# Where the conversion of the weights runs: 24 steps in row 0 instead of 36, the rest over all of row 1, and one token group of channel work moved to row 2

## The chip, the cores and the metric

The kernel runs on one core of one Trainium2 chip. The metric is the device time of one execution in microseconds (us). Three runs of the kernel before took 1360.92, 1362.69 and 1366.38 us; the median, 1362.69 us, is what a change is compared with. One more execution was profiled: the program ran 1362.23 us and the profile spans 1360.1 us of it.

The core has five engines with an instruction queue each. PE is the matrix engine, DVE the vector engine, ACT the scalar engine with activation functions, POOL the general engine (GpSimd) and SP the engine that here only issues transfers (DMA). Each works through its queue in the order of the program. An instruction waits until the data and the buffers that it needs are free, and all that stands behind it on its engine waits too.

## The reference

The input is an attention block with 8 batch elements, 8 heads, 576 tokens and 64 numbers per head, followed by an MLP mixer:

```python
scores = scale * (q @ k.T)                          # per batch element and head, 576 x 576
scores = where(scores >= max(scores) - tau, scores, -1e9)
attn = softmax(scores)
x = heads side by side of (attn @ v)                # 8 x 576 x 512
u = x + (relu(x.T @ w_tok1) @ w_tok2).T             # mixing over the 576 tokens, width 256
out = u + relu(u @ w_ch1) @ w_ch2                   # mixing over the 512 channels, width 1536
```

q, k and v are float32. The four weight matrices are float64, and the kernel computes in float32, so it has to convert them on the chip. That conversion is what the change moves.

## The kernel before

**Rows and units.** A "row" is one batch element, `b` from 0 to 7. A row is cut into 18 "units", so that there are 144, and the main loop (from L572) takes one unit per turn; `u` is its number, so units 18 to 35 are row 1. A unit is 128 query rows of one pair of heads. For unit u the loop emits, spread over engines:

- `scores(u)` (L289): 8 matmuls into PSUM on PE (line L303), two maxima on DVE (L308), two small instructions on POOL that make the threshold (L309);
- `weigh(u)` (L312): threshold and exponential on ACT (L318, L325);
- `norm(u - 1)` (L329): two tiny DVE instructions (L332, L333) and two scalings on POOL (L336);
- for unit w = u - 2 the transposition of the attention weights. In row 0 that is `turn` on PE with copies on DVE and ACT (L354, L356). From row 1 on it is `turn_blocks` (L358): one DVE transpose in blocks of 32 x 32 (L366, tile T), and after every third unit 16 transfers that move the blocks to their places (L375, tile eT), all issued by SP;
- `values` (L392): attention times v (L410, L415, tile pv), once for every three units. From row 1 on it is emitted at the end of the unit two after the one in which the 16 transfers were issued, and so directly ahead of the next unit's scores on PE.

**The mixer as filling.** When a row's attention is complete, `push` (L537) appends its mixer work to a list `todo`: `token_mlp` (L427), then `channel_mlp` (L476) for groups of 256 tokens. A group has 12 steps `ch1` of the first layer (8 matmuls each in the records, L487) and, for each of its two blocks of 128 tokens, 4 steps `ch2` of the second layer (L499, L503, with a copy on DVE, L508, at the end). `fill(share)` (L524) takes steps from the list at fixed places in the next row's units, by their estimated costs: a unit may take `quota`. `push` sets the quota so that `KEEP` of the list's cost is left after a row: 45 after rows 1 to 7, `KEEP_FIRST` = 20 after row 0. Row 0's list has two groups. `push(0)` runs in unit 20, `push(1)` in unit 39.

**The conversion.** The weights are cut into 31 pieces of up to 128 x 512 numbers: 3 of w_tok1, 4 of w_tok2, 12 of w_ch1, 12 of w_ch2. Each piece is loaded as 64-bit words by SP (`load_piece`, L177) into one of 4 raw buffers, and converted by two ACT instructions (L192, L194), three DVE instructions (L202, L204, L208) and one POOL addition (L216), which also frees the raw buffer. The sequence is cut into 94 steps, `weight(n)` (L224): step 3i is the first DVE instruction of piece i with the POOL addition of piece i - 1 and the load of piece i + 3; steps 3i + 1 and 3i + 2 are the other two DVE instructions with the ACT instructions of piece i + 1. `weight_to(x)` makes steps until x are done. `need(i)` (L242) makes as many as a piece requires before a step of the mixer uses it.

**What sets the order.** The order on each engine is the order in which the loop emits instructions; nothing reorders them later. In a unit of row 0 weight steps come in two places, and the target grows by 2.25 steps a unit (L599, L634). From unit 18 on `weight(2)` stands in three places of a unit (L595, L623, L629): after `norm`, after `turn_blocks`, and after `weigh`:

```python
if b_now:
    weight(2)
else:
    weight_to(2.25 * (u - (1 if visit else 1.5)))
```

On SP the loads of weights, the loads of v and, in row 0, the loads of q and k (L105) stand in one queue with the 16 transfers of each group of three units. From row 1 on q and k are loaded from ACT's queue.

Of the kernel before, what the change touches and what calls it, by code (L numbers as in the profile page):

```python
# [9 lines left out]
F32 = mybir.dt.float32  # L10
# [7 lines left out]
P = 128  # L18
# [3 lines left out]
def kernel(  # L22
# [38 lines left out]
    NCC = DM // P  # L61
# [16 lines left out]
    ps_mm = None  # L78
# [7 lines left out]
    UB = 9 * NP // 2  # L86
# [81 lines left out]
    def load_piece(i):  # L168
        if i >= len(pieces):
            return  # L170
        dst, src = pieces[i]
        rows = dst.shape[0]
        n = 1
        for d in dst.shape[1:]:
            n *= d
        raw = raw_at[i % NRAW][0:rows, 0 : n * (2 if wide(i) else 1)].bitcast(src.dtype)
        nc.sync.dma_start(out=like(raw, dst), in_=src)  # L177
        if wide(i):
            words = raw.bitcast(U32).rearrange("p (n w) -> p n w", w=2)
            h2 = work.tile([P, WMAX], F32, tag="o", name=f"h2_{i}")[0:rows, 0:n]  # L180
            raws[i] = like(words[:, :, 0], dst), like(words[:, :, 1], dst), like(h2, dst)
        else:
            raws[i] = like(raw, dst)
# [4 lines left out]
    def on_scalar(i, part):  # L188
        if wide(i):
            lo, hi, h2 = raws[i]  # L190
            if part == 0:
                nc.scalar.activation(out=lo.bitcast(I32), in_=lo, func=AF.Copy, scale=2.0**-29)  # L192
            else:
                nc.scalar.activation(out=h2, in_=hi.bitcast(F32), func=AF.Abs)  # L194
# [17 lines left out]
    def on_gpsimd(i):  # L212
        if i >= 0:
            dst = pieces[i][0]
            if wide(i):
                nc.gpsimd.tensor_tensor(out=dst.bitcast(I32), in0=dst.bitcast(I32), in1=raws.pop(i)[0].bitcast(I32), op=ALU.add)  # L216
            else:
                nc.gpsimd.tensor_copy(out=dst, in_=raws.pop(i))
# [5 lines left out]
    def weight(n):  # L224

        nonlocal steps_done
        for k in range(steps_done, min(steps_done + n, 3 * len(pieces) + 1)):
            i, part = divmod(k, 3)
            if part == 0:
                on_gpsimd(i - 1)  # L230
                if i:
                    load_piece(i - 1 + NRAW)
            else:
                on_scalar(i + 1, part - 1)
            on_vector(i, part)
            steps_done = k + 1

    def weight_to(x):

        weight(max(int(x) - steps_done, 0))  # L240

    def need(i):  # L242

        weight(3 * i + 4 - steps_done)
# [32 lines left out]
    def in_blocks(b):  # L277
        return b > 0
# [197 lines left out]
    def channel_mlp(b, uT, i):  # L476

        s = {}
        n = min(GR, 2 * S - GR * i)

        def ch1(j):
            need(7 + j)
            if j == 0:
                s["g"] = work.tile([P, NJ, GR], F32, tag="g", bufs=1, name=f"g_{b}_{i}")
            ps = ps_mm.tile([P, GR], F32, tag="mm", name=f"c1_{b}_{i}_{j}")[:, 0:n]
            for c in range(NCC):
                nc.tensor.matmul(ps, lhsT=wc1[:, j, c, :], rhs=uT[:, c, GR * i : GR * i + n], start=(c == 0), stop=(c == NCC - 1))  # L487
            nc.scalar.activation(out=s["g"][:, j, 0:n], in_=ps, func=AF.Relu)  # L488

        def ch2(t, part):  # L490
            need(7 + NJ + 3 * part + 2)
            t0 = GR * i + P * t
            if part == 0:
                s["ps"] = ps_mm.tile([P, NCC, P], F32, tag="mm", name=f"c2_{b}_{i}_{t}")
            ps = s["ps"]
            flat = ps.rearrange("q c d -> q (c d)")
            if part == 0:
                for c in range(NCC):
                    nc.tensor.matmul(  # L499
                        ps[:, c, :], lhsT=uT[:, c, t0 : t0 + P], rhs=ident, is_transpose=True, start=(c == 0), stop=False, skip_group_check=True  # L500
                    )
            for j in range(3 * part, 3 * part + 3):
                nc.tensor.matmul(  # L503
                    flat, lhsT=s["g"][:, j, P * t : P * t + P], rhs=wc2[:, j, :], start=False, stop=(j == NJ - 1), skip_group_check=True
                )
            if part == 3:
                o = work.tile([P, DM], F32, tag="o", name=f"o_{b}_{i}_{t}")
                nc.vector.tensor_copy(out=o, in_=flat)  # L508
                nc.sync.dma_start(out=out[b : b + 2].rearrange("b s d -> (b s) d")[t0 : t0 + P, :], in_=o)

        return [(0.0067 * n, lambda j=j: ch1(j)) for j in range(NJ)] + [
            (2.6 if part else 3.0, lambda t=t, part=part: ch2(t, part)) for t in range(n // P) for part in range(4)
        ]

    KEEP = 45.0
    KEEP_FIRST = 20.0
    todo = deque()  # L520
    quota = 0.0
    credit = 0.0
# [14 lines left out]
    def push(b):  # L537
# [13 lines left out]
        for i in range(2) if b % 2 == 0 else range(2, (2 * S + GR - 1) // GR):  # L551
            todo.extend(channel_mlp(b - b % 2, uT, i))
        quota = (sum(c for c, _ in todo) - (KEEP if b else KEEP_FIRST)) / (UB - 1)

    prep(0)
    due = deque()
    b_now = 0
    LAG = 2

    def values_due(u):  # L560
        while due and due[0][0] <= u:
            _, b, p0, g = due.popleft()
            values(b, p0, g)
            if b == 0 and p0 == 0 and g == 2:
                return True
            if p0 == NP - 2 and g == 2:
                if not in_blocks(b):
                    return True
                push(b)
        return False  # L570

    for u in range(len(units) + LAG + 4):  # L572
        on = u < len(units)
        if u == UB:
            late.close()
            ps_mm = ctx.enter_context(tc.tile_pool(name="ps_mm", bufs=2, space=bass.MemoryType.PSUM))
        if on:
            b_now, p0, t = units[u]
            n = b_now * NP + p0
        w = u - LAG  # L580
        back = 0 <= w < len(units)
        if on:
            scores(u)

        last = False
        visit = False
        if due and not in_blocks(due[0][1]):
            visit = due[0][0] <= u
            last = values_due(u)
        elif early:  # L590
            early.popleft()[1]()
        if 0 < u <= len(units):
            norm(u - 1)
        if b_now:
            weight(2)  # L595
        else:


            weight_to(2.25 * (u - (1 if visit else 1.5)))  # L599
            if visit and on:  # L600
                weigh(u)
        while copies:
            copies.popleft()()
        if last and u < UB:
            early.extend(token_mlp(0, range(NP // 2))[0])
        elif last:
            push(0)
        if back:
            wb, wp, wt = units[w]
            if not in_blocks(wb):  # L610
                for i in range(3):
                    turn(w, i)
            if wt % GU == GU - 1:
                g = wt // GU
                if g < 2:
                    split_middle(wb * NP + wp + g)
                due.append((u + (2 if in_blocks(wb) else 1), wb, wp, g))
        if b_now:
            fill(0.4)
        if back and in_blocks(wb):  # L620
            turn_blocks(w)
        if b_now:
            weight(2)  # L623
        if on and (b_now or not visit):
            weigh(u)
        elif b_now:
            fill(0.6)
        if b_now:
            weight(2)  # L629
        elif u == 0:  # L630
            on_scalar(0, 0)
            on_scalar(0, 1)
        else:
            weight_to(2.25 * (u - 1))  # L634
        if on:


            when = {3: (2, 0, 2), 4: (2, 2, 4), 5: (2, 4, 6), 6: (2, 6, 8), 8: (3, 0, 3), 0: (1, 3, 6), 1: (1, 6, 8)}
            if u == 0:
                load_qk(1, (nc.sync, nc.sync), range(0, 3))  # L640
            if t in when:
                m, lo, hi = when[t]
                if n + m < len(pairs):
                    load_qk(n + m, (nc.scalar if b_now else nc.sync,) * 2, range(lo, hi))
            if t in (3, 7) and n + 2 + t // 4 < len(pairs):
                load_v(n + 2 + t // 4)
            if t == 2:
                prep(n + 1)
            if t == 7 and n + 2 < len(pairs):
                prep(n + 2)  # L650
        if due and in_blocks(due[0][1]):
            values_due(u)
# [31 lines left out]
```

## Time and profile before

| What | Value |
|---|---|
| median of 3 runs | 1362.69 us |
| span of the profiled execution | 1360.1 us |
| PE busy | 1315.2 us, 97% of the span |
| DVE, ACT, POOL busy | 575.3, 584.3, 353.6 us (42, 43, 26%) |
| row 0: start to the first scores of unit 18 | 0 to 99.76 us, PE busy 78.30 of the first 100 us |
| row 1: scores of unit 18 to scores of unit 36 | 99.76 to 240.55 us |
| conversion instructions on DVE (L202, L204, L208) | 31 each, the last begins at 187.2 us |
| channel layers, matmuls of L487 and L503 | 400.3 and 390.6 us busy |
| mean of one issue of a transfer of L375 (median) | 602 ns, 672 of them |
| such a transfer from its issue to landing (median) | 2.3 us |

The busy time of PE is modelled from the starts of pipelined matmuls, so that short waits inside a group of matmuls don't show as idle time; the length of a whole group (8 matmuls of scores take 1.24 us where nothing disturbs them) tells more. "Idle before" beside an instruction is the time that its engine sat before it, and the name behind the arrow is what came last by the profile, which need not be what was waited for.

### The profile page before, as it was taken

The numbers are of one execution on the slowest core, as the hardware profiler recorded it, in microseconds if no ns is written. First come the engines' busy times: TensorE is split into PE (matmuls) and PEld (weight loads), VectorE is DVE, ScalarE is ACT, GpSimd is POOL, SyncE is SP. The second block draws the span as 40 slices with busy tenths as digits, with TensorE's granted clock in tenths as the row PEclk, the third lists the DMA queues.
The fourth block names the chain that finished last, engine by engine and source line by source line (L and its number), as shares of the span: only waits on it lengthen the run. The fifth ranks groups of instructions, "written<-read, shape, count | busy, mean of one in ns | idle before, by whom it ended". The sixth has DMA issues, their size and how long they took to land.

```text
span 1360.1 us, 17717 instructions
## 1 busy us (share of the span) xinstructions
PE 1315.2 (97%) x6246; PEld 817.2 (60%) x6246; DVE 575.3 (42%) x1009; ACT 584.3 (43%) x1299; POOL 353.6 (26%) x683
## 2 busy tenths in 40 slices
PE   6888899999999999999999999999999999999998
PEld 4555556547474666655665566565756566576675
DVE  5878874445443434443333454434333443201000
ACT  6776664445454444543434445353434444120010
POOL 4666653222222222221212222222212222100000
PEclk9999999999999999999999999999999999999999
DMA  5434774545453533533244444435333442400000
GB/s 122 109 92 129 196 170 102 127 95 127 96 130 77 134 89 84 135 76 92 66 112 99 104 97 114 95 76 118 90 90 74 114 99 70 111 0 16 8 16 16
DMA packets 278871, 128.20 MB, mean 94 GB/s; under 512 B 200896, under 2 KB 271552, under 8 KB 278784
## 3 DMA queue, kind: packets, MB, share of 16 engines
q1 hardware_dynamic: 150176, 111.06, 32.0%
q10 hardware_dynamic: 128608, 16.01, 7.4%
q8 instruction: 50, 0.82, 0.3%
q14 instruction: 37, 0.30, 0.1%
HBM read 43.25 MB, written 9.44 MB: 39 GB/s over the span
## 4 chain that ended last, share of the span: by engine, by line
PE 89%; DVE 4%; DMA 2%; ACT 2%; issue 1%; SPq 1%; POOL 1%; ACTq 0%; DVEq 0%; POOLq 0%
PE c L503 28%; PE c L487 27%; PE sc L303 11%; PE pv L415 8%; PE t L453 5%; PE t L463 4%; PE pv L410 3%; DVE mx L308 2%; PE c L499 1%; PE tx L446 1%; PE tr L354 1%; ACT e L318 1%; SPq L375 1%; DMA eT<-T 1%; DMA lk<-in_k_dram 1%
## 5 line engine op out<-in xcount | busy, mean ns | idle before, releaser
L308 DVE TENSOR_REDUCE mx<-sc 128x1 f32<-128x576 f32 x288 | 204.5, 750 | 484.6 <-PE sc L303 484.6
L487 PE MATMUL c<-xT,wc 128*128 128x256 f32 (+1 forms) x1920 | 400.3, 362 | 0.1
L503 PE MATMUL c<-wc,g 128*128 128x512 f32 x864 | 390.6, 597 | 0.0
L487 PEld LDWEIGHTS c<-xT,wc 128*128 128x128 f32 x1920 | 334.4, 191 | 70.5 <-issue 31.5
L309 POOL TENSOR_SCALAR bias<-mx,toff 128x1 f32<-128x1 f32 x288 | 81.9, 284 | 781.2 <-DVE mx L308 724.3
L318 ACT ACTIVATE e<-sc,bias 128x576 f32<-128x576 f32 x288 | 199.4, 740 | 157.5 <-POOL bias L309 153.5
L503 PEld LDWEIGHTS c<-wc,g 128*128 128x128 f32 x864 | 157.4, 190 | 175.4 <-issue 173.7
L488 ACT ACTIVATE g<-c 128x256 f32<-128x256 f32 (+1 forms) x240 | 86.8, 362 | 321.4 <-PE c L487 308.6
L325 ACT ACTIVATE e<-e,ntau 128x576 f32<-128x576 f32 x288 | 221.1, 772 | 0.0
L336 POOL TENSOR_SCALAR e<-e,rr 128x576 f32<-128x576 f32 x288 | 214.6, 757 | 14.7 <-DVE rr L333 2.8
L303 PE MATMUL sc<-kT,qT 64*128 64x288 f32 (+1 forms) x1280 | 193.5, 441 | 11.9 <-DVE kT L285 7.2
L366 DVE STREAM_TRANSPOSE T<-e 128x1152 f32<-128x1152 f32 x126 | 172.1, 1366 | 5.8 <-DMA eT<-T 3.6
L303 PEld LDWEIGHTS sc<-kT,qT 64*128 64x128 f32 (+1 forms) x1280 | 106.2, 181 | 99.2 <-issue 61.8
L415 PE MATMUL pv<-eT,lv 128*64 128x384 f32 (+1 forms) x1024 | 136.2, 406 | 0.0
L415 PEld LDWEIGHTS pv<-eT,lv 128*64 128x64 f32 x1024 | 75.2, 137 | 49.3 <-issue 40.4
L508 DVE COPY o<-c 128x512 f32<-128x512 f32 x36 | 24.7, 687 | 169.7 <-PE c L503 169.7
L420 ACT COPY xT<-pv 128x384 f32<-128x384 f32 (+1 forms) x56 | 21.0, 400 | 166.2 <-PE pv L415 165.2
L463 PE MATMUL t<-w,a 128*128 128x288 f32 x256 | 73.6, 414 | 5.7 <-DVE xT L467 4.8
L453 PE MATMUL t<-x_sb,w 128*128 128x512 f32 (+1 forms) x180 | 73.4, 555 | 0.0
L467 DVE TENSOR_TENSOR xT<-xT,t 128x288 f32<-128x288 f32 x64 | 28.4, 448 | 86.6 <-PE t L463 86.0
L463 PEld LDWEIGHTS t<-w,a 128*128 128x128 f32 x256 | 45.5, 190 | 28.0 <-issue 11.7
L325 ACT ACTIVATION_READ_ACCUMULATOR e<-e,ntau 128x1 f32 x288 | 56.8, 197 | 0.0
(44 smaller groups left out, 547.2 us busy)
## 6 DMA issues: line engine op xcount, KB each, us to landing
eT<-T SPq DMA_DIRECT2D x672, 108.0 KB, 2.3
scratch<-in_moe_w_ch_dram SPq DMA_DIRECT2D x24, 512.0 KB, 3.8
lv<-in_v_dram SPq DMA_DIRECT2D x32, 288.0 KB, 3.5
out_dram<-o SPq DMA_DIRECT2D x36, 256.0 KB, 2.2
lk<-in_k_dram ACTq DMA_DIRECT2D x111, 72.0 KB, 2.7
lq<-in_q_dram ACTq DMA_DIRECT2D x106, 72.0 KB, 2.3
lq<-in_q_dram SPq DMA_DIRECT2D x22, 72.0 KB, 3.2
lk<-in_k_dram SPq DMA_DIRECT2D x17, 72.0 KB, 3.4
```

What stands on the lines that cost most here:

```text
L303: nc.tensor.matmul(sc[h][rows, f, 0:HS], lhsT=qT[r, cols], rhs=kT[r, HS * f : HS * f + HS], start=True, stop=True)
L308: nc.vector.tensor_reduce(out=mx[:, c], in_=sc[h][:, :, 0:HS], axis=AX.XY, op=ALU.max)
L318: nc.scalar.activation(out=eh, in_=sc[h][:, :, 0:HS], func=AF.Prelu, bias=bias[:, h : h + 1], scale=SCALE, alpha=STEEP)
L325: nc.scalar.activation(out=eh, in_=eh, func=AF.Exp, bias=ntau, accum_out=rs[:, h : h + 1])
L336: nc.gpsimd.tensor_scalar(out=eh, in0=eh, scalar1=rr[:, h : h + 1], scalar2=1.0, op0=ALU.mult, op1=ALU.mult)
L366: nc.vector.transpose(out=T[:, :, place, :].rearrange("p a (c x) -> p c a x", c=NK), in_=e.rearrange("p (c a x) -> p c a x", c=NK, a=4))
L415: nc.tensor.matmul(to[r], lhsT=lv[:, j, :], rhs=e[j], start=False, stop=(c == NI - 1), skip_group_check=True)
L453: nc.tensor.matmul(to, lhsT=w1[:, t, P * m : P * m + P], rhs=x_sb[:, t, cols], start=(t == 0), stop=(t == NT - 1))
L463: nc.tensor.matmul(to, lhsT=a[:, m, P * c : P * c + P], rhs=w2[:, m, HS * f : HS * f + HS], start=(m == 0), stop=(m == NTK - 1))
L487: nc.tensor.matmul(ps, lhsT=wc1[:, j, c, :], rhs=uT[:, c, GR * i : GR * i + n], start=(c == 0), stop=(c == NCC - 1))
L488: nc.scalar.activation(out=s["g"][:, j, 0:n], in_=ps, func=AF.Relu)
L503: nc.tensor.matmul(flat, lhsT=s["g"][:, j, P * t : P * t + P], rhs=wc2[:, j, :], start=False, stop=(j == NJ - 1), skip_group_check=True)
```

## The change

Four things are changed together.

1. Row 0 makes 1.75 steps a unit instead of 2.25, and stops at `WROW` = 24. The kernel before was at 36 when row 1 began.
2. In row 1 the three calls `weight(2)`, 6 steps a unit, become a target that grows by `WRATE` = 4 steps a unit, with its steps at the same three places: two steps after `norm`, one after `turn_blocks`, one after `weigh`. Step 94 is thus reached in unit 35 instead of unit 27.
3. `KEEP_FIRST` goes from 20 to 42, so that row 1 takes less of row 0's list: the first group of tokens is done in it, the second one later.
4. For group 0 of row 0 the second layer is sorted by weights: part 0 of both blocks of tokens, then part 1 of both, and so on, so that late pieces are needed late. For that both blocks hold a PSUM buffer at once, `s[t]` instead of `s["ps"]`.

```diff
-                s["ps"] = ps_mm.tile([P, NCC, P], F32, tag="mm", name=f"c2_{b}_{i}_{t}")
-            ps = s["ps"]
+                s[t] = ps_mm.tile([P, NCC, P], F32, tag="mm", name=f"c2_{b}_{i}_{t}")
+            ps = s[t]
...
+        last = [(t, part) for t in range(n // P) for part in range(4)]
+        if b == 0 and i == 0:
+            last.sort(key=lambda x: x[1])
         return [(0.0067 * n, lambda j=j: ch1(j)) for j in range(NJ)] + [
-            (2.6 if part else 3.0, lambda t=t, part=part: ch2(t, part)) for t in range(n // P) for part in range(4)
+            (2.6 if part else 3.0, lambda t=t, part=part: ch2(t, part)) for t, part in last
         ]
...
-    KEEP_FIRST = 20.0
+    KEEP_FIRST = 42.0
...
+    WROW = 24
+    WRATE = 4.0
...
         if b_now:
-            weight(2)
+            weight_to(WROW + WRATE * (u - UB))
         else:
-            weight_to(2.25 * (u - (1 if visit else 1.5)))
+            weight_to(min(1.75 * (u - (1 if visit else 1.5)), WROW))
...
         if b_now:
-            weight(2)
+            weight_to(WROW + WRATE * (u - UB + 0.4))
...
         if b_now:
-            weight(2)
+            weight_to(WROW + WRATE * (u - UB + 0.7))
...
         else:
-            weight_to(2.25 * (u - 1))
+            weight_to(min(1.75 * (u - 1), WROW))
```

## The prediction

> **What bounds the kernel now.** I read the page's slices first, then busy times by stretch, then the queues of SP, PE and DVE in order of time through row 1.
>
> ```profile
> PE   6888899999999999999999999999999999999998
> ...
> DVE  5878874445443434443333454434333443201000
> ...
> PEclk9999999999999999999999999999999999999999
> ```
>
> A slice is 34 us. PE is short of work only in the first five slices, which are row 0 and the start of row 1; there DVE is at 0.5 to 0.8. Cut at the first scores of unit 18 (99.76), and at the starts of the transfers of units 22 and 40 on SP:
>
> ```profile
> core 0: us, PE busy (x) PEld busy (x) DVE busy (x) ACT busy (x) POOL busy (x), PEclk, DMA share, GB/s
> 99.76:142.03 42.27, 34.50 (x166) 22.46 (x166) 36.65 (x65) 26.89 (x55) 25.19 (x31) 0.92 0.50 137
> 142.03:277.10 135.07, 129.08 (x618) 78.67 (x617) 80.88 (x133) 72.04 (x157) 55.51 (x91) 0.99 0.59 143
> 277.10:1360.00 1082.90, 1073.57 (x5003) 666.93 (x5002) 383.78 (x652) 412.14 (x935) 216.92 (x463) 1.00 0.36 85
> ```
>
> Up to 142 DVE is the fuller engine (36.65 of 42.27). From 277 on PE has 9 us of idle time in 1083, so PE work moved there costs its full length. The stretch between is the one to understand: PE is 96% busy, but something else turns over in step with it. It is SP's queue:
>
> ```profile
> 142.03 10.98 SPq L375 DMA_DIRECT2D eT<-T  x16
> ...
> 169.69 10.42 SPq L375 DMA_DIRECT2D eT<-T  x16
> ...
> 191.23 10.30 SPq L375 DMA_DIRECT2D eT<-T  x16
> ...
> 212.19 11.66 SPq L375 DMA_DIRECT2D eT<-T  x16
> ...
> 233.43 12.99 SPq L375 DMA_DIRECT2D eT<-T  x16
> ```
>
> Every three units SP issues 16 transfers one after another, for 10.3 to 13.0 us. The attention times v of those units comes after:
>
> ```profile
> 225.73 0.87 PE L410 MATMUL pv<-eT,vl 128*64 128x384 f32 x4 [0.78 <-issue]
> ...
> 229.11 1.24 PE L303 MATMUL sc<-kT,qT 64*128 64x288 f32 x8
> ...
> 248.65 0.55 PE L410 MATMUL pv<-eT,vl 128*64 128x192 f32 x4 [1.92 <-DMA lq<-in_q_dram]
> ```
>
> Blocks ending at 153.01, 223.85 and 246.42 are followed by pv at 155.06, 225.73 and 248.65: 2.05, 1.88 and 2.23 us later, one landing (median 2.3), with PE idle before them. PE arrives at the same time as the data or earlier. So in row 1 there is a ring: block of transfers, pv, next scores (behind pv on PE), maximum, block transpose T, next block. PE's filling lies beside it.
>
> **What the Trainium skill says.** "DMA: Bandwidth & Descriptors", section "Issuing engines are not separate DMA queues": issuing from several engines only saves the sequencer's time, "usually small relative to the DMA itself". Here it isn't small: 16 issues at a median 0.602 us are 10 us against one landing of 2.3, so the number of issues sets the ring. "SBUF — State Buffer", section "Who interferes with whom": VectorE and GpSimd share a port pair that one instruction holds whole. The trace agrees: L204 takes 0.44 us at 138.68 and 1.48 at 142.84, begun 0.1 us after POOL's 1.30 us addition L216. "TensorE: Matmul & The Clock Gate", section "HAM oscillation — how this bites in real kernels": gaps of over some 3.4 us bring the array back to half clock. The trace shows clock 0.92 in 99.76 to 142.03 and 1.00 after 277; I use it for a rival.
>
> **The change, part by part.** A unit is told by its scores. Signs are seen from the time of the same unit.
>
> *(a) Before the block of unit 22: fewer steps.* There the kernel before has made 62 steps, the changed one 40 (24 + 4 x 4), with the ACT, POOL and load instructions of each. Row 0 loses 12. From 36 to 99.76 us the DVE lines L202, L204, L208 have 16.3 us in 27 instructions, 0.60 each; 12 x 0.60 = 7.2, of which I count the share that DVE is busy, 53 of 64 us: 6.0. Units 18 to 22 lose 10; from 99.76 to 142 the same lines have 19.0 us in 27, 0.70 each, so 7.0. PE's own chain through units 20 and 21 (pv 3.4, the token layers) would be next, so I take 6.5. Together -12.5. Bounds: -8 if ACT's copies and PE's transposes hold row 0 rather than DVE; -20 if all 22 steps count at 0.70 (15.4) and some 4 us of SP's waiting goes too, where in row 0 q and k stand behind loads that wait for POOL.
>
> *(b) From the block of unit 22 to that of unit 40: the ring.* 135.07 us before, six turns. Its parts after the change: block to landing 2.05; pv 3.4 (225.73 to the scores at 229.11); scores to maximum 1.27 (207.88 to 209.14); and from the maximum to the next block. In the changed order two steps stand between maximum and T in units 25, 28 and 31 (L208, L202), then comes T, and the load that belongs to L202's step stands ahead of the block on SP and waits for POOL. Unit 22 of the kernel before has just this:
>
> ```profile
> 136.64 1.42 DVE L308 TENSOR_REDUCE mx<-sc 128x1 f32<-128x576 f32 x2
> 137.97 0.16 DVE L332 TENSOR_SCALAR rr<-rs 128x2 f32<-128x2 f32 x1
> 138.16 0.17 DVE L333 RECIPROCAL rr<-rr 128x2 f32<-128x2 f32 x1
> 138.24 0.41 DVE L202 TENSOR_SCALAR h<-h 128x512 f32<-128x512 f32 x1
> 138.68 0.44 DVE L204 TENSOR_SCALAR wc<-h 128x512 uint32<-128x512 uint32 x1
> 139.04 0.81 DVE L467 TENSOR_TENSOR xT<-xT,t 128x288 f32<-128x288 f32 x2
> 139.77 1.36 DVE L366 STREAM_TRANSPOSE T<-e 128x1152 f32<-128x1152 f32 x1
> ```
>
> POOL scales until 140.37, adds until 141.62, SP loads at 141.65 and the block starts at 142.03: 5.4 us after the maximum. In unit 34 no load is left in front, only the two steps (1.0) beside T: 4.1. With the blocks' own lengths (11.0, 10.4, 10.3, 11.7) the turns are 11.0 + 2.05 + 3.4 + 1.27 + 5.4 = 23.1, then 22.5, 22.4 and 11.7 + 6.7 + 4.1 = 22.5. The last two, from unit 34 on, have no steps before T and stay as they were before, 22.9 and 20.7, less 0.8 together for PE's smaller load. Sum 133.4; against 135.07 that is -1.7. The other loads of weights, now about four between two blocks, stand behind a block and before the next, where SP has some 9 us of slack. So a ring that PE's filling had just covered is not shortened by taking filling away. In a turn PE would have 3 x 1.2 scores + 3.4 pv + 3 x 3.04 filling, 1.05 us for a unit of cost (1.80 for an L487 step put at 1.715), = 16.6 us of work in 22.5, and DVE 3 x (1.33 + 0.5 + 1.3) + 12 steps at 0.70 + 1 = 18.8: neither fills it. Bounds -8 and +6, a little over 1 us a turn.
>
> *(c) PE work that leaves this stretch.* The list costs 93.7; quota goes from 73.7 / 17 = 4.34 to 51.7 / 17 = 3.04 a unit. By the scores of unit 40 the kernel before has done group 1's 12 first-layer steps and 6 of 8 second-layer parts; the changed one 6 first-layer steps. Missing: 6 x 1.80 (x24 take 5.4) + 6 x 2.70 (x12 take 5.35) + 2 x 0.44 for L499 = 27.9. It is done after unit 40, where PE has no room: +27.9. Only the gaps right there, 1.47 us before L446 and 1.78 before L463 between 282 and 308, take some of it, since the left-over steps are laced between the token steps: -3.2. Bounds: +22 (more gaps filled) to +28.
>
> *(d) Edits at nothing.* The sort and `s[t]` hold both PSUM buffers from unit 30 to 35, when no other step asks for one; the copy L508 that frees the first comes a part ahead of the next `ch1`. Loads of pieces run 7 steps ahead, 1.75 units instead of 1.2, so ACT's 18.6 us of waiting for them in row 1 shrinks; (b) contains that, since the ring goes on beside it.
>
> Sum: -12.5 - 1.7 + 27.9 - 3.2 = +10.5. On the span of 1360.1 that is 1370.6; the median run stands 2.6 over that span, so 1373.2.
>
> **The rivals.**
> *The ring doesn't bind (ends faster).* If the blocks were issued faster or pv didn't wait for them, DVE would set the pace, 18.8 + some 0.4 = 19.2 a turn: 18 us less in six turns, 1355. For: four of the six turns before were 20.7 to 21.5, close to that. Against: those had no steps or load before T, and 10.3 + 2.05 + 3.4 + 1.27 alone are 17.0. It decides from 20.5 us a turn downward (10.5 / 6 below the mean 22.2).
> *The start gains all it can.* (a) at -19: 1366. For: SP's waits for POOL in row 0 stand in the chain of waits. Against: DVE isn't full there.
> *The idle PE pays more.* If each turn's 6 us gap on PE brings half clock, pv and scores (4.6 us) take up to 1.7 us more, and weight steps held by POOL lengthen the way to T: 2 to 3 us a turn in five turns, 1385. For: 0.92 above. Against: the gap of 3.04 us at 136.5 left the clock at 1.00 afterwards.
>
> **How the numbers follow.** Likeliest 0.58, its own range 1366 to 1381; ring not binding 0.15 (1350 to 1360); large start 0.15 (1361 to 1370); idle PE 0.12 (1381 to 1391). For 8 in 10 I take 1357 to 1386. Half a per cent, 6.8 us, is about what a measurement of this kernel can tell from no change: 1355.9 and 1369.5. Below: two thirds of the second, a little of the third, 0.12. Above: 0.7 of the likeliest, a quarter of the third, all of the last, 0.57. Within: 0.31.
>
> **What would show it.** (a) The scores of unit 18 at about 94 instead of 99.76, the block of unit 22 at about 129.5. (b) Blocks of units 22 to 34 spaced 22 to 23.5 us, each pv 2 us after its block ends, PE idle several us before each, DVE with idle time before the maxima of units 25, 28 and 31. (c) PE at 0.75 to 0.85 from 130 to 260 and full after it; some 25 us more PE work after unit 40. It is wrong if the blocks come every 20 us, or if the block of unit 22 starts before 122.

## The result and the profile after

| | kernel before | changed kernel |
|---|---|---|
| median (6 runs each on one chip) | 1361.99 us (1360.92 to 1366.38) | 1386.91 us (1384.86 to 1389.06) |
| ratio, 95% interval | | 1.0177 (1.0160 to 1.0195) |
| span of the profiled execution | 1360.1 us | 1387.3 us |

The change costs 24.9 us by the medians, 27.2 us between the two profiled executions. That of the changed kernel (1389.06 us) is the slowest of its six runs, 2.2 us above their median, so the figures cut from its profile hold some 2 us more than the medians do. The forecast was 1373.2 us, slower by about 10.5, with a range up to 1386. Slower was right; the loss is more than twice as large and the median lies 0.9 us above the range.

The page's slices of the changed kernel (35 us each):

```profile
PE   6898886899999999999999999999999999999998
...
PEclk9999998999999999999999999999999999999999
```

PE is now short of work until slice 8, three slices longer than before, and its clock sinks in slice 7: a place that was full has room now. Cut at the same events as before (first scores of unit 18; transfers of units 22 and 40 on SP):

```profile
core 0: us, PE busy (x) PEld busy (x) DVE busy (x) ACT busy (x) POOL busy (x), PEclk, DMA share, GB/s
0.00:95.89 95.89, 77.04 (x465) 48.93 (x465) 65.23 (x148) 68.65 (x146) 48.28 (x97) 1.00 0.45 99
95.89:131.01 35.12, 31.26 (x164) 20.25 (x164) 30.49 (x56) 25.53 (x53) 21.09 (x27) 1.00 0.41 103
131.01:276.14 145.13, 115.64 (x534) 68.67 (x533) 95.94 (x154) 77.26 (x162) 72.58 (x98) 0.91 0.60 155
276.14:1387.30 1111.16, 1101.49 (x5089) 684.20 (x5087) 384.33 (x653) 415.67 (x941) 216.91 (x463) 1.00 0.36 83
```

| Stretch | before | after | difference | predicted |
|---|---|---|---|---|
| start to scores of unit 18 | 99.76 | 95.89 | -3.9 | -6 |
| to block of unit 22 | 42.27 | 35.12 | -7.2 | -6.5 |
| block of unit 22 to block of unit 40 | 135.07 | 145.13 | +10.1 | -1.7 |
| to the end | 1083.00 | 1111.16 | +28.2 | +24.7 |

Read the third row with PE's busy time: 129.08 us in 135.07 before, 115.64 in 145.13 after. Less work was done in this stretch, and it took longer. Nearly everything that was won at the start (11.1) was lost again here, so that unit 40's block starts at 276.14 instead of 277.10. The missing 27.9 us of PE work (1101.49 - 1073.57) then follow in a stretch in which PE has no room.

The turns of the ring, as SP's queue shows them:

```profile
131.01 10.48 SPq L375 DMA_DIRECT2D eT<-T  x16
...
154.15 11.13 SPq L375 DMA_DIRECT2D eT<-T  x16
...
177.73 12.73 SPq L375 DMA_DIRECT2D eT<-T  x16
...
204.66 10.41 SPq L375 DMA_DIRECT2D eT<-T  x16
...
227.16 12.35 SPq L375 DMA_DIRECT2D eT<-T  x16
...
253.34 11.07 SPq L375 DMA_DIRECT2D eT<-T  x16
```

and PE's side of three of them, in order of time:

```profile
192.15 1.55 PE L410 MATMUL pv<-eT,vl 128*64 128x384 f32 x4 [6.27 <-DMA eT<-T]
193.46 4.07 PE L415 MATMUL pv<-eT,lv 128*64 128x384 f32 x16
197.46 1.20 PE L303 MATMUL sc<-kT,qT 64*64 64x288 f32 x16
...
215.82 1.38 PE L503 MATMUL c<-wc,g 128*128 128x512 f32 x2 [3.13 <-POOL wc L216]
217.18 1.54 PE L410 MATMUL pv<-eT,vl 128*64 128x384 f32 x4
...
235.80 3.78 PE L503 MATMUL c<-wc,g 128*128 128x512 f32 x4 [6.07 <-POOL wc L216]
...
245.63 0.55 PE L410 MATMUL pv<-eT,vl 128*64 128x192 f32 x4
```

Two things are to be seen. After an idle time of 6.27 us pv takes 5.3 us (192.15 to the scores at 197.46), where the kernel before took 3.4. The clock in windows of 4 us says why:

```profile
188.00:192.00 4.00, 0.00 (x0) 0.66 0.75 172
192.00:196.00 4.00, 3.85 (x12) 0.50 0.93 335
```

(columns: PE busy with its instructions, PEclk, DMA share, GB/s). And PE, idle on average, is late where it counts: the block of unit 34 ended at 239.51, and pv came at 245.63, since the second layer ahead of it had waited 6.07 us for a piece of weights.

Each turn can be cut into four parts from these two queues: the block's length; from its end to pv; pv, up to the next scores; and from those scores to the next block.

| Turn from block at | block | to pv | pv | scores to block | turn | predicted |
|---|---|---|---|---|---|---|
| 131.01 | 10.48 | 2.03 | 3.38 | 7.25 | 23.1 | 23.1 |
| 154.15 | 11.13 | 1.83 | 3.40 | 7.22 | 23.6 | 22.5 |
| 177.73 | 12.73 | 1.69 | 5.31 | 7.20 | 26.9 | 22.4 |
| 204.66 | 10.41 | 2.11 | 4.74 | 5.24 | 22.5 | 22.5 |
| 227.16 | 12.35 | 6.12 | 3.40 | 4.31 | 26.2 | 22.9 less a little |
| 253.34 | 11.07 | 2.36 | 5.07 | 4.30 | 22.8 | 20.7 less a little |
| sum | 68.2 | 16.1 | 25.3 | 35.5 | 145.1 | 133.4 |
| over the prediction's parts | +1.5 | +3.7 | +4.9 | +1.5 | +11.7 | |

For the last row the two turns that the prediction took over whole are cut as the kernel before shows them (12.99 + 2.23 + 3.40 + 4.32, and 10.29 + 2.76 + 3.38 + 4.30), and the 0.8 is taken from the way to pv.

This table measures against the prediction. Against the kernel before, whose columns cut in the same way add up to 66.6, 15.3, 22.5 and 30.7 us, the +10.1 of the stretch are +1.5, +0.8, +2.8 and +4.9. The largest part lies between the scores and the next block, where steps and loads of the conversion now stand in four turns (7.2 and 5.2 us) and stood in one before (9.1 us, 4.3 in the other five); the prediction had counted 3.4 of these 4.9. The first turn is 4.5 us shorter than before (27.7), the other five are 14.6 us longer together.

### The profile page after: what moved, and what is told of

It reads as the page before. It is cut to its first block, busy times and chain, and to the rows that moved or that the text cites. A ratio compares the mean times of both kernels' runs of the same rounds, so it can differ in the third digit from the quotient of the medians.

```text
span 1387.3 us, 17698 instructions
## 1 busy us (share of the span) xinstructions
PE 1325.4 (96%) x6246; PEld 822.0 (59%) x6246; DVE 576.0 (42%) x1009; ACT 587.1 (42%) x1299; POOL 358.9 (26%) x683
## 4 chain that ended last, share of the span: by engine, by line
PE 85%; DVE 4%; DMA 3%; SPq 3%; ACT 2%; issue 1%; POOL 1%; DVEq 0%; POOLq 0%
PE c L503 25%; PE c L487 25%; PE sc L303 11%; PE pv L415 9%; PE t L453 5%; PE t L463 4%; PE pv L410 3%; SPq L375 3%; DVE mx L308 2%; DMA eT<-T 1%; PE tr L354 1%; PE tx L446 1%; PE c L499 1%; ACT e L318 1%; DMA scratch<-in_moe_w_ch_dram 1%
## 5 line engine op out<-in xcount | busy, mean ns | idle before, releaser
L503 PE MATMUL c<-wc,g 128*128 128x512 f32 x864 | 393.6, 600 | 11.0 <-POOL wc L216 11.0
L503 PEld LDWEIGHTS c<-wc,g 128*128 128x128 f32 x864 | 157.9, 190 | 188.1 <-issue 170.6
L415 PE MATMUL pv<-eT,lv 128*64 128x384 f32 (+1 forms) x1024 | 139.3, 414 | 0.0
L508 DVE COPY o<-c 128x512 f32<-128x512 f32 x36 | 24.8, 689 | 179.3 <-PE c L503 179.3
L410 PE MATMUL pv<-eT,vl 128*64 128x384 f32 (+1 forms) x256 | 46.0, 436 | 18.9 <-DMA eT<-T 15.7
```

What stands on the lines that cost most here:

```text
L410: nc.tensor.matmul(to[r], lhsT=vl[:, r], rhs=e[NI], start=True, stop=False, skip_group_check=True)
L415: nc.tensor.matmul(to[r], lhsT=lv[:, j, :], rhs=e[j], start=False, stop=(c == NI - 1), skip_group_check=True)
L503: nc.tensor.matmul(flat, lhsT=s["g"][:, j, P * t : P * t + P], rhs=wc2[:, j, :], start=False, stop=(j == NJ - 1), skip_group_check=True)
```

## The experiments

A row of figures behind a run is: median, ratio to the kernel before on the same chip with its 95% interval, and the length of the stretch from the block of unit 22 to that of unit 40 (135.1 before, 145.1 after).

### Is taking away filling enough to lose the time? (e1)

```diff
 (kernel before)
-    KEEP_FIRST = 20.0
+    KEEP_FIRST = 42.0
```

> The kernel before with one edit: KEEP_FIRST 42 instead of 20; the conversion stays as it was. Theory (ring of transfers, PE work at full price later): 27.9 us of PE work leave the stretch between the transfer blocks of units 22 and 40, the blocks stay 20.5 to 23 us apart, so that stretch gains at most 6 us, and the work is paid after it: 1384 us, 1378 to 1390. Rival (the moved filling is neutral, what costs is that the conversion is spread and its pieces come late): 1359 to 1366.

1394.49 us, 1.0245 (1.0224 to 1.0265), stretch 140.3. The kernel before with this one number changed is slower than the changed kernel. Its profiled span is 33.8 us longer: 2.2 up to unit 22's block, 5.3 in the stretch, 26.3 after it. So nearly all of the loss after unit 40 (28.2 in the changed kernel) comes with KEEP_FIRST alone, and a stretch freed of PE work became longer, not shorter, with no weight step moved. It was 4 us above the theory's range, for the same reason as the forecast: the stretch had been expected to keep its length. In four of its six turns it takes 4.9 to 6.2 us from pv to the next scores. In one of these the scores wait for ACT, as they did in the kernel before (there 5.55 us); in the other three pv runs at half clock after idle times of 3.8 to 4.2 us, as here:

```profile
274.05 1.55 PE L410 MATMUL pv<-eT,vl 128*64 128x384 f32 x4 [4.15 <-DMA eT<-T]
275.35 4.97 PE L415 MATMUL pv<-eT,lv 128*64 128x384 f32 x16
280.26 1.20 PE L303 MATMUL sc<-kT,qT 64*64 64x288 f32 x16
```

pv takes 28.1 us in the six turns, against 22.5 before: these 5.6 us are as much as the stretch gains in length, and no late piece or moved step is among their causes.

### Does the later conversion bear the filling of before? (e2, e8)

```diff
 (e2, changed kernel)
-    KEEP_FIRST = 42.0
+    KEEP_FIRST = 20.0
```

> The changed kernel with one edit: KEEP_FIRST back at 20, so that the filling of row 1 is as before, while the conversion starts row 1 at 24 steps and goes on at 4 steps a unit or as fast as the filling demands it. Theory (ring and full price): the 27.9 us come back, the gain of some 11 us before unit 22 stays, and PE is full beside the ring again: 1352 to 1364. Rival (spread and late pieces cost): 1375 to 1387.

1396.24 us, 1.0257 (1.0236 to 1.0278), stretch 176.7: a miss for both theories. The filling is back, and after unit 40 the profile takes 1083.4 us, as before the change. But the stretch is 31.5 us longer than in the changed kernel: the second layer now waits 23.3 us for POOL's pieces (11.0 in the changed kernel), the first layer 3.6, and in the turns of units 25 and 28 pv comes 15.8 and 28.8 us after the block's end. With 4 steps a unit the pieces of weights don't come at the pace at which a full quota asks for them. So KEEP_FIRST alone (e1, 1.0245) and the later conversion with its sort alone (e2, 1.0257) each cost more than the two together (1.0177).

```diff
 (e8, kernel before: row 0's part alone, 6 steps a unit afterwards)
-            weight_to(2.25 * (u - (1 if visit else 1.5)))
+            weight_to(min(1.75 * (u - (1 if visit else 1.5)), 24))
...
-            weight_to(2.25 * (u - 1))
+            weight_to(min(1.75 * (u - 1), 24))
```

> The kernel before with the change in row 0 alone: 1.75 steps a unit up to 24, then 6 steps a unit and KEEP_FIRST 20 as before, so that the conversion ends in unit 29 instead of 27. Theory: row 0 gains its 4 us (scores of unit 18), and the 12 steps fall into units 27 to 29, where the ring and PE's filling leave DVE idle: 1356 to 1362. Rival (the steps are paid in row 1, and pieces come late for the second layer in units 27 to 29): 1363 to 1370.

1372.78 us, 1.0065 (1.0040 to 1.0091), stretch 150.5: a miss again, on the slow side. Unit 22's block starts 4.3 us earlier (137.75), and the stretch is 15.5 us longer: the 12 steps moved out of row 0 cost more in the ring than the 8.4 us (12 x 0.70) that DVE needs for them, and PE waits 5.7 us for late pieces, where it had waited for none. In the turn of unit 28 pv comes 13.0 us after its block. The gain in row 0 is thus not kept here either, where the quota is that of before.

### Does the ring bind, and how much does a block's length count? (e3, e4)

```diff
 (e3 changed kernel, e4 kernel before; one eT for the whole run)
-                for i in range(4):
+                for i in range(4 if u < 26 or u > 42 else 2):
```

Half of the 16 transfers of the blocks of units 28 to 40 are left out, and with them half of those attention weights.

> The changed kernel with 8 instead of 16 transfers in the blocks of units 28, 31, 34, 37 and 40 (half of the attention weights of those groups is not moved, the tile keeps older values there; the tile eT is allocated once). Theory (ring): a block takes 5 to 6 us instead of 10.4 to 12.7, each turn from unit 28 to 40 falls to about 20 us, where DVE's work with its weight steps is next, so 4 turns save 3 to 6 us each and PE's half-clock stretches go: 1366 to 1374. Rival (late pieces: PE's L503 waits for POOL's L216, 11 us in all, hold the stretch): 1380 to 1387, and those waits stay.

> The kernel before with 8 instead of 16 transfers in the same five blocks (half of the attention weights of those groups is not moved). Theory: here PE's filling covers the ring, with only 0.8 and 1.9 us of idle time before two pv, so shorter blocks gain little: 1357 to 1362. Rival (the ring alone sets the pace before the change too): 4 turns of 3 us and more, 1345 to 1352.

e3: 1373.79 us, 1.0088 (1.0072 to 1.0105); e4: 1357.96 us, 0.9968 (0.9957 to 0.9979). Both times lie in the theory's range. The stretches:

```profile
130.31:259.79 129.48, 109.82 (x534) 66.14 (x533) 95.97 (x154) 77.09 (x162) 72.73 (x98) 0.95 0.58 147
```

```profile
144.35:275.36 131.01, 129.55 (x623) 78.33 (x622) 81.76 (x133) 72.23 (x157) 55.59 (x91) 1.00 0.50 120
```

The same edit takes 15.6 us from the stretch of the changed kernel (first line) and 4.1 from that of the kernel before (second), where PE is then busy for 129.55 of 131.01 us: there PE bounds it as well as the ring. The blocks' own lengths fall by 22.8 and 24.8 us in sum. In the changed kernel most of that is gained, so there the ring sets the pace. Not all came as the theory had it: the clock is still 0.95, and the second layer still waits 10.6 us for late pieces, as the rival said, so that the turn of unit 34 stays at 25.8 us.

### Has PE room there? (e5, e12)

```diff
 (e5 changed kernel, e12 kernel before: first layer of row 0's group 0 computed twice, the second time over the first)
-            for c in range(NCC):
-                nc.tensor.matmul(ps, ..., start=(c == 0), stop=(c == NCC - 1))
+            for _ in range(2 if b == 0 and i == 0 else 1):
+                for c in range(NCC):
+                    nc.tensor.matmul(ps, ..., start=(c == 0), stop=(c == NCC - 1))
```

> The changed kernel, but each of the 12 first-layer steps of group 0 of row 0 (units 23 to 29) runs its matmuls twice, the second time over the first: 21.6 us more PE work in the stretch, nothing else. Theory (the ring sets the pace and PE has room beside it): the time stays within 5 us of the changed kernel's 1387, or falls by up to 5 us because PE keeps its full clock there; the blocks of units 22 to 31 stay where they were. Rival (PE's work counts in row 1): about 1387 + 15 to 22 = 1402 to 1409.

> The kernel before with the twelve first-layer steps of row 0's group 0 multiplied twice, +21.6 us of TensorE work in the same place as in the changed kernel, where it cost 2 us. Theory (before, TensorE is full beside the ring, and work added there is paid): 1376 to 1384. Rival (there is slack in the ring before, too): 1362 to 1369.

e5: 1388.80 us, 1.0186 (1.0164 to 1.0207), stretch 147.4; by the ratios it can't be told from the changed kernel (1.0177). e12: 1377.21 us, 1.0099 (1.0084 to 1.0114), stretch 149.1, 13 us above the kernel before. Both theories held by the time.

```profile
129.92:277.35 147.43, 131.63 (x630) 83.22 (x629) 96.23 (x154) 77.75 (x162) 72.83 (x98) 0.92 0.60 153
```

```profile
142.42:291.48 149.06, 146.58 (x714) 94.89 (x713) 81.39 (x133) 72.89 (x157) 55.94 (x91) 1.00 0.53 129
```

With 96 more instructions PE is 16.0 us busier in the changed kernel's stretch (first line against 115.64), which grows by 2.3; in that of the kernel before it is 17.5 us busier (against 129.08), and the stretch grows by 14.0. The room in the changed kernel is not wholly free: in the first two turns pv comes 4.3 and 3.7 us after the block instead of 2.0 and 1.8, and these turns are 3.5 us longer together. The third is 2.7 us shorter, since pv is back at 3.4 us there and the block takes 10.9 instead of 12.7. This is the clearest view of what the change did: the work that it took out would cost little where it was, and it put it where there is no room (26.3 us in e1).

### Do the late pieces count? (e7, e6, e14)

```diff
 (e7, changed kernel)
-        if b == 0 and i == 0:
-            last.sort(key=lambda x: x[1])
 (e6, changed kernel)
-    WRATE = 4.0
+    WRATE = 4.6
 (e14, changed kernel, in all three places)
-            weight_to(WROW + WRATE * (u - UB))
+            weight_to(WROW + WRATE * (u - UB) + 2 * max(u - UB - 12, 0))
```

> The changed kernel without the sort: the second layer of group 0 goes block of tokens by block again, so its fourth part, which needs the last piece, comes in unit 31 and draws 18 steps of the conversion together there. Theory (pieces that are late hold PE, and through it the pv and the ring): 1390 to 1398. Rival (the order of the second layer is neutral): 1385 to 1389.

> The changed kernel with WRATE 4.6 instead of 4: the last step in unit 33 instead of 35, so that pieces come about two units earlier at the end. Theory A (late pieces are part of the loss: PE's second layer waited 11 us for POOL's additions in units 33 and 35, which held the pv of unit 36 for 4 us): those waits go, 1378 to 1384. Theory B (only the ring and the moved work): 1385 to 1389.

> The changed kernel with the conversion at 6 steps a unit instead of 4 from unit 30 on, unchanged until then, so that row 1's last pieces come before the second layer asks for them. Theory (late pieces lengthen the turn of unit 34): the 11.0 us for which the second layer waits for pieces fall below 4, the turn 26.2 falls to 22 to 23.5, at a cost of up to 1 us in the turn of unit 31: 1383 to 1385. Rival (the added steps stand before maximum and T and take the gain): 1386 to 1390.

e7, without the sort: 1398.72 us, 1.0265 (1.0236 to 1.0294), stretch 154.3. The sort is worth some 12 us in the changed kernel; without it pieces are asked for earlier than they are there, and in the turn of unit 31 pv comes 16.3 us after the block instead of 2.1. e6: 1386.11 us, 1.0158 (1.0124 to 1.0192), stretch 142.3, no shorter time that could be told. The wait for L216 has gone from the second layer and the last turns are shorter, but the first three take 74.9 us instead of 73.7. e14 makes as many steps as the changed kernel until unit 30, and then 6 a unit. In its profiled execution the turn of unit 34 takes 21.1 us instead of 26.2, even less than the theory says, at 1.4 us more in the turn before, with pv 1.98 us after the block's end instead of 6.12:

```profile
131.31:270.24 138.93, 114.82 (x534) 70.08 (x533) 94.86 (x154) 76.95 (x162) 71.68 (x98) 0.91 0.63 162
```

That span is 1381.3 us, 6.0 below the changed kernel's. The timed runs don't bear it out: 1385.61 us, 1.0177 (1.0149 to 1.0205), the same ratio as the changed kernel's. The profiled execution of e14 (1383.32 us) is the fastest of its five, that of the changed kernel the slowest of its six, and this choice makes most of the 6.0 us. That late pieces make this turn longer is shown; that the whole kernel gets faster without them is not.

### Is the half clock a cause? (e9, e10, e13, e15)

Extra multiplications, whose result pv overwrites, keep PE at work while it waits for a block.

```diff
 (changed kernel, ahead of pv)
+        if b == 1:                       # e13: b == 1 and g == 2, and 5 instead of 8
+            for _ in range(8):
+                nc.tensor.matmul(whole[:, 0:384], lhsT=ident, rhs=vals[b * NP + p0][0][:, 0:6, :], ...)
```

e10 is e9 with the edit of e6, e15 is e13 with that of e14.

> The changed kernel with eight extra TensorE multiplications of 128x384 (some 0.45 us each, 3.6 us) ahead of each of row 1's six pv groups; pv overwrites what they leave. They fill part of the idle time in which TensorE waits for the block. Theory (in the ring, half clock after idle time stretches pv: 5.3, 4.8 and 5.3 us instead of 3.4 in three turns, 4.7 to 5.2 in all): pv is back at 3.4 in these turns, the stretch from the block of unit 22 to that of unit 40 falls from 145.1 to 138 to 142, 1379 to 1384. Rival (the clock is a by-product; the turn is set by the blocks' own lengths and by late pieces): pv may be shorter but the blocks come no earlier, 1386 to 1390.

> The same extra multiplications, and the conversion at 4.6 steps a unit in row 1 instead of 4.0, so that pieces are ready before the second layer asks. Theory (late pieces and half clock both lengthen the ring, and each shows only when the other is gone): the 142.3 of rate 4.6 alone falls to 133 to 138, 1375 to 1381. Rival (more conversion steps between maximum and block cost what they give): 141 to 145, 1384 to 1389.

> The changed kernel with five extra TensorE multiplications of 128x384 (0.66 us each, 3.3 in all) ahead of two of row 1's pv groups alone, those where TensorE stands idle for 6.3 and 4.1 us and pv then takes 5.3 and 5.1 us. Theory (the half clock is a cause of the longer turn): both pv back at 3.4, the stretch from the block of unit 22 to that of unit 40 falls from 145.1 to 141 to 142.5, 1382 to 1385. Rival (something else takes the time up, a turn is as long as before): 144.5 or more, 1386 to 1389.

> Both edits together. Theory (they are separate causes and add): the stretch from the block of unit 22 to that of unit 40 at 136.5 to 139.5, 1378 to 1382. Rival: no lower than the better of the two alone.

e9: 1397.70 us, 1.0250 (1.0234 to 1.0267). All six pv are back at 3.4 us, but the eight multiplications took 5.3 us (7.2 once) and not 3.6, and ended after the blocks had landed: from a block's end to pv it takes 33.4 us in the six turns instead of 16.1. They cost more than they could bring; the time lies above both theories' ranges and doesn't tell them apart. e10, with the same fault: 1387.65 us, 1.0179 (1.0155 to 1.0202), stretch 148.3; outside the theory's range too.

e13 put five of them (3.39 us) in the two turns alone that had the room. There it worked: the two pv take 3.4 us and these turns 24.9 and 21.5 us instead of 26.9 and 22.8. But in this execution half clock met the pv of the first two turns, which have no edit and whose pv had been at full clock before; PE stood idle ahead of their pv for 3.46 and 2.89 us, instead of 1.11 and 2.35:

```profile
146.77 1.55 PE L413 MATMUL pv<-eT,vl 128*64 128x384 f32 x4 [3.46 <-DMA eT<-T]
148.08 3.61 PE L418 MATMUL pv<-eT,lv 128*64 128x384 f32 x16
151.61 1.24 PE L303 MATMUL sc<-kT,qT 64*128 64x288 f32 x8
```

They took 25.3 and 25.8 us instead of 23.1 and 23.6, of which 1.5 and 1.7 are pv. The stretch is 146.2, the time 1387.90 us, 1.0186 (1.0158 to 1.0214): by the time, the rival's. e15: 1387.55 us, 1.0174 (1.0145 to 1.0203), stretch 140.5 in its profile, no sum of two gains. How long PE stands idle in a turn, and where half clock follows, varies from one execution to the next, and a cure for two places is no cure for the ring. So a pv at half clock is longer by up to 2 us, as the turns show one by one; what the whole kernel would gain at full clock stays open.

### Would two queues issue a block faster? (e11)

```diff
 (changed kernel)
-                    nc.sync.dma_start(out=eT[32 * a : 32 * a + 32, :, i, :], ...)
+                    (nc.sync if i < 2 else nc.scalar).dma_start(out=eT[32 * a : 32 * a + 32, :, i, :], ...)
```

> The changed kernel with 8 of a block's 16 transfers issued from ScalarE's queue and 8 from SyncE's. Nothing is left out. Theory (16 issues on one queue are the largest part of the ring): each block is 4 to 6 us shorter, 20 us over the stretch less what ScalarE pays, 1368 to 1378. Rival (ScalarE waits for the block transpose with its exponentials queued behind the issues, and these lead to the next block): the turns stay at 23 to 25 us, 1383 to 1392.

1697.65 us, 1.2443 (1.2419 to 1.2467): a miss by far. Two blocks of row 1, each with its half in SP's queue and its half in ACT's:

```profile
162.37 7.90 SPq L375 DMA_DIRECT2D eT<-T  x8
...
258.63 6.80 SPq L375 DMA_DIRECT2D eT<-T  x8
```

```profile
160.35 7.47 ACTq L375 DMA_DIRECT2D eT<-T  x8
...
258.58 6.33 ACTq L375 DMA_DIRECT2D eT<-T  x8
```

In row 1 eight issues on SP take 6.8 to 8.1 us when ACT issues too; three of the four blocks of eight from SP alone in e3 took 5.2 to 5.6, the fourth 7.2. In the first four blocks ACT begins some 2 us ahead of SP, and a block lasts 9.3 to 10.1 us from the first issue to the last (the first one shown from 160.35 to 170.27), little less than from one queue. In the other three both begin together, and a block lasts 6.8 to 6.9 us (258.58 to 265.43) against 10.4 to 12.7 in the changed kernel. So two queues did issue a block faster there; the time is lost elsewhere. What the edit costs is on ACT (waits of ACT, by line and releaser: sum, times, longest):

```profile
ACT e L318 <- DMA eT<-T: 333.8, 36, 13.1
```

The exponentials of the units that follow stand behind the issues on ACT, and these stand until T is made and eT, of which there is one, has been read by pv. This waiting is 333.8 us, against 4.3 in the changed kernel, and is of the size of the whole loss (310.7). It is not shown to be all of it: PE, which waits in its turn, is at a mean clock of 0.91 and busy for 108 us longer. The rival had the mechanism but not its size: it had only looked at the ring of row 1, and this wait goes on through all rows.

## Why the prediction was wrong

*(a) Fewer steps before unit 22's block*: -11.1 against -12.5, right in sum. Row 0 gave 3.9 instead of 6.0, the rest 7.2 instead of 6.5. The rest went with a clock of 1.00 instead of 0.92 (PE busy 31.26 us instead of 34.50, with two instructions fewer), which the prediction had not counted, so that the 7.2 are not shown to be DVE's steps alone. The "large start" rival (-19) was not met.

*(b) The ring*: this is the step that failed, +10.1 against -1.7. The idea was right: "a ring that PE's filling had just covered is not shortened by taking filling away" is what e1, e3 and e5 show. That the first turn came to a tenth of a microsecond is in part luck: its block was 0.5 us shorter than put, its way from scores to block 0.6 longer. The way from scores to block, with the two steps before T and the load in front, took 7.2 in three turns where 6.67 had been put. What failed is the assumption that the other parts keep the length they had in a full PE: pv was put at 3.4 in every turn and the way to it at one landing, both read while PE was busy. The way was read behind three blocks only; behind the other three of the kernel before (ends 180.11, 201.53 and 266.66) pv came 3.40, 2.98 and 2.76 us later, with PE at work up to it, so that "PE arrives at the same time as the data or earlier" did not hold for half of the turns. pv took 25.3 instead of 20.4 us in six turns, at half clock in three of them, and the way to pv 16.1 instead of 12.4. The first is half clock; of the second, 3.7 us, most is the turn in which the second layer ahead of pv waits for a late piece.

The rival "the idle PE pays more" had the half clock and said 1385; it got 0.12. Its other half, weight steps on the way to T, is only the +1.5 of the fourth column, and the late piece ahead of pv it did not have, so that its figure came closer than its reasons. It was turned down by one gap of 3.04 us that had left the clock at 1.00. The idle times that the same prediction worked out for PE, 6 us a turn, were twice that, and the one observation could not speak for them. Nor did it speak for shorter ones: in the same profile half clock had followed idle times of 2.10 us (ahead of the scores at 160.61) and 2.63 us (at 113.91).

*(c) PE work that leaves the stretch*: +27.9 was exact to the digits shown (1101.49 - 1073.57 = 27.9). The 3.2 us to be recovered in gaps behind unit 40 were not: PE's idle time there is 9.7 us after and 9.4 before, since new waits took the place of the old ones. The gaps that the prediction named are gone; others came, 1.77 us before pv at 457.00 and 1.89 at 1214.76. e1 shows 26.3 of it from KEEP_FIRST alone.

*(d) Edits at nothing*: half wrong. The sort cost nothing and is worth 12 us (e7). That later pieces cost nothing was wrong: the second layer waits 11.0 us for POOL's additions, L503's idle time in the page being 0.0 before. The wait in the turn of unit 34, ahead of pv, fell on the ring with its length: the 3.7 us above. One of 3.13 us (ahead of 215.82) stands before one of the three pv at half clock. The prediction asked where the pieces' loads stand, and did not set the last of them (step 94, unit 35) against the units in which the second layer asks for them.

*The rival on the faster side* (a ring that doesn't bind, 20.5 us a turn or less) was not met: no turn after is under 22.5. e3 does take turns down to 16.9 us; what bounded them was the blocks, not DVE.

In sum: +1.4 from (a), +11.8 from (b) and (d), +3.5 from (c) make the 16.7 us between the forecast's +10.5 and the profile's +27.2.

## What to carry to other kernels

Work that fills the wait of a chain of latencies costs little there (2.3 us for 16.0 in e5) and nearly its full length where the engine is full (14.0 for 17.5 in e12): before moving it, measure what the place is worth by doubling some of it, as e5 and e12 do. When filling leaves a chain, don't keep the durations read while the engine was full: price its links once at half clock, and set each late operand against the time at which it will be asked for. A gain at the head of a chain counts only if the chain then runs at its old pace.

## What the runs showed of the hardware that was not expected

- Two queues that issue small transfers at once each take longer for an issue, 0.85 to 1.0 us on SP in row 1 of e11 instead of 0.65 to 0.7 alone (three of four blocks of eight, e3; 0.9 in the fourth). A block that both begin together is still out sooner, in 6.9 us.
- Half clock came after every idle time of PE of 3.13 us and more between 100 and 280 us in the two kernels' profiles (3.13, 4.09, 6.07 and 6.27 us), and stayed for some 3.5 us or twice that. Of the shorter ones of over 1.5 us, those of 1.99 (ahead of 133.99), 2.47 (157.36), 2.10 and 2.63 us (160.61 and 113.91 in the kernel before) were followed by it too, those of 2.35 (167.11), 1.92 and 3.04 us (248.65 and 139.54 in the kernel before) were not. The Trainium skill ("TensorE: Matmul & The Clock Gate", section "HAM oscillation — how this bites in real kernels") puts the limit at gaps of over some 3.4 us. The longer cases agree with that; the shorter ones show that here the length of a single gap doesn't decide it.
